# Moving the first tile's mask products to PE, with new load order, weight pieces and buffer counts, in a block-sparse attention and feed-forward kernel

## The chip, the cores and the metric

The kernel runs on one core of a Trainium2 chip. The metric is device time in microseconds (us) of the slowest core, here the only one, as the median of several executions. Before the change it was 276.54 us (three runs, 276.49 to 277.82). The engines are named as the profile names them: PE (matrix multiplications), PEld (PE's weight loads, which overlap PE), DVE (vector), ACT (scalar, exponentials and tanh), POOL (general purpose), SP (here only the issuer of the hardware load queue).

## The reference, cut to what matters

```python
batch, n_heads, seq, head_dim = 4, 8, 768, 64;  block = 32           # attention
n_tokens, d_model, d_ff = 3072, 512, 2048                            # feed-forward
scores = (1 / sqrt(64)) * matmul(q, k.transpose(0, 1, 3, 2))
mask = abs(blk_i - blk_j) <= 1  |  first or last block row or column
for qb in range(24):                       # and three drawn blocks of k in each block row
    for kb in sampled_blocks[qb]: mask[block qb, block kb] = True
attn = softmax(where(mask, scores, -1e9))
x = matmul(attn, v).transpose(0, 2, 1, 3).reshape(3072, 512)
h = x @ w_in;  g = h * sigmoid(beta * h);  out = g @ w_out           # float32 in and out
```

## The kernel before

The kernel writes down all its work as a list of nodes with an engine, a cost and dependences. A greedy scheduler then deals them out, once, while the program is recorded, and what comes out is a fixed order for each engine. An engine works through its list in order: if its next instruction must wait, everything behind it waits too (below, five loads wait behind one that is issued only at 13.42 us).

A *unit* is one pair of heads and one tile of queries (256 or 512). For each unit: loads of k, q and v (float32, into staging buffers `st_k`, `st_q`, `st_v`), casts to float16 on DVE or POOL, transposes on PE, score matmuls on 64 rows (PE), exponential (ACT), a product with a 0/1 mask (DVE), attention times V (PE, 65 columns), normalisation (DVE), a transpose of x. When all four pairs of a tile have their x, the feed-forward of that tile follows: matmuls with `w_in`, tanh (ACT), gate product (DVE), matmuls with `w_out`.

```python
SLOTS = {"st_k": 2, "st_q": 5, "st_v": 5, "s16_k": 4, "s16_q": 2, "set": 4, "va": 4,
         "et": 13, "xst": 5, "recip": 7, "t_sb": 6, "g": 2, "osb": 3, "sc": 4}   # buffers of each kind

def ex(eng, sc=sc, et=et):                              # one step: exponential of 128 x 1024 scores
    act.activation(out=at(et)..., in_=at(sc)..., func=AF.Exp, bias=0.0, scale=SCALE)

def mk(eng, et=et, kc0=kc0):                            # and its mask product
    dve.tensor_tensor(out=e, in0=e, in1=m, op=ALU.mult)

def load():                                             # all loads: one list, on SP
    ... nc.sync.dma_start(out=o, in_=hg)
last_load[:] = [add("load", "SP", ..., load, deps=..., take=[st])]      # takes a staging buffer

def shut():                                             # weights may start when pair 3's k has landed:
    nc.gpsimd.tensor_copy(out=w_in_sb[0:1, 0, 0:1], in_=at(st)[0:1, 0, 0:1])     # one element of it
... nc.gpsimd.dma_start(out=w_in_sb[...], in_=w_in_r[...])              # 2 + 2 pieces, issued by POOL
```

Batch 0 has four pairs of heads, numbered 0 to 3. Their loads go out in this order, where k0, q0, v0 belong to pair 0, k0a to k0c are thirds of k0, and r0 to r3 are the second halves (512 queries) of each pair's q:

```
k0a q0 k0b k0c v0 k1 q1 v1 k2 q2 v2 k3 q3 v3 r0 r1 r2 r3
```

The softmax here doesn't subtract the row's maximum and nothing guards it: scores larger than these inputs give would overflow.

Of the kernel before, what the change touches and what calls it, by code (L numbers as in the profile page):

```python
# [23 lines left out]
class Node:  # L24


    def __init__(self, kind, eng, dur, lat, emit, deps=(), take=(), use=(), moved=0,
# [13 lines left out]
BIAS = {"av": -69, "beta": -455, "cast": 94, "dma": -1239, "ex": 257, "gm": -727, "hp": -468,  # L41
        "load": 1496, "lone sc": 331, "mask": -1415, "mk": 241, "next sc": 94, "norm": -152,
        "op": -13, "op on": -70, "osb": 284, "sc": -204, "spread": -316, "th": 422,
        "turn": -3422, "turn cp": -88, "two sc": -72, "weights": 774, "x cp": -31,
        "x turn": -102}

W_GATE = (3, "k")
# [12 lines left out]
MOST = {"av": 8, "hp": 6, "sc": 3}  # L60
# [180 lines left out]
def kernel(  # L241
# [29 lines left out]
    SLOTS = {"st_k": 2, "st_q": 5, "st_v": 5, "s16_k": 4, "s16_q": 2, "set": 4, "va": 4,  # L271
             "et": 13, "xst": 5, "recip": 7, "t_sb": 6, "g": 2, "osb": 3, "sc": 4}
# [36 lines left out]
    onehot = persist.tile([NB, NG, P], FP16, name="onehot")  # L309
    mask16 = persist.tile([NB, NB], FP16, name="mask16")  # L310
# [26 lines left out]
    def emit_first():  # L337
# [6 lines left out]
        nc.vector.memset(warm, 0.0)  # L344

# [7 lines left out]
        nc.gpsimd.memset(onehot, 1.0)  # L353
        nc.gpsimd.affine_select(out=onehot, in_=onehot, pattern=[[CG * P, NG], [CG, P]],
                                compare_op=ALU.is_ge, fill=0.0, base=0,
                                channel_multiplier=-BLK)
        nc.gpsimd.affine_select(out=onehot, in_=onehot, pattern=[[-CG * P, NG], [-CG, P]],
                                compare_op=ALU.is_ge, fill=0.0, base=BLK - 1,
                                channel_multiplier=BLK)
# [22 lines left out]
    mask_of = {}  # L382

    def add_mask():
# [3 lines left out]
        def mb(eng):  # L388
            dve.tensor_copy(out=sb_f32, in_=sb_i32)
            for r in range(3):  # L390
                dve.scalar_tensor_tensor(out=mask_blk if r < 2 else mask16, in0=iota_j,
                                               scalar=sb_f32[:, r:r + 1], in1=mask_blk,
                                               op0=ALU.is_equal, op1=ALU.max)

        def mt():
            pe.matmul(at(tb)[0:NB, 0:NB], lhsT=mask16, rhs=identity[0:NB, 0:NB],
                             start=True, stop=True)
# [4 lines left out]
        def km():  # L402
            for g in range(NG):
                pe.matmul(at(kb)[:, g * NB:(g + 1) * NB], lhsT=onehot[:, g], rhs=mask_t,
                                 start=True, stop=True)
# [20 lines left out]
        n_mt = add("mask", "PE", 60, 200, mt, deps=[n_mb], take=[tb], rows=32)  # L426
        n_mtc = add("mask", ("ACT", "DVE"), {"ACT": 200, "DVE": 100}, 100, mtc, deps=[n_mt], use=[tb])
# [16 lines left out]
    def add_weights(gate):  # L444
        st, load = gate

        def shut():
            nc.gpsimd.tensor_copy(out=w_in_sb[0:1, 0, 0:1], in_=at(st)[0:1, 0, 0:1])
        gate = add("weights", "POOL", 600, 50, shut, deps=[load], use=[st])
        for i in range(2):  # L450
            def wi(i=i):
                nc.gpsimd.dma_start(out=w_in_sb[:, :, i * 1024:(i + 1) * 1024],
                                    in_=w_in_r[:, :, i * 1024:(i + 1) * 1024])
            w_in_of[i] = add("weights", "POOL", 1000, 0, wi,
                            deps=[gate if i == 0 else (w_in_of[0], -1e9)], moved=2097152, port=True)
# [279 lines left out]
    for x in range(NPAIR):  # L735
        add_rest(x)
# [74 lines left out]
```

## Time and profile before

| | before |
|---|---|
| median, three runs | 276.54 us |
| PE, DVE, ACT busy | 259.7, 209.2, 217.1 us of a profiled span of 275.0 |
| PE work, added up from start-to-start times | 250.3 us |
| end of the last matmul | 270.6 us, so PE lost 20.2 us |
| of these lost by 31.3 us / by 62 us | 16.4 / 19.7 us |
| first feed-forward matmul | 30.18 us |

"Lost" needs a word, because PE's busy share does not show it: a matmul that runs at half clock, or is drawn out by modelled ends, counts as busy. I added up what the PE stream needs at its usual spacing, read from the trace: 216 ns for a 512-column matmul, 109.5 for 256, 56 for 128, 32 for an attention-times-V matmul of 65 columns, 217 or 110 ns for a pair of 64-row score matmuls, and 96 ns at each change between 64 and 128 rows. Time elapsed less that sum is what PE lost.

The page of the kernel before; first busy time, share and instruction count, then the busy tenths in 40 slices of 6.9 us, then the chain that ended last:

```profile
PE 259.7 (94%) x2455; PEld 139.7 (51%) x2455; DVE 209.2 (76%) x416; ACT 217.1 (79%) x284; POOL 32.5 (12%) x53
...
PE   6677899969999999999999999999999999999993
...
PEclk9999999999999999999999999999999999999999
...
PE 88%; DVE 5%; ACT 2%; DMA 2%; SPq 1%; issue 1%; ACTq 0%; DVEq 0%
```

PE is full from slice 10 on. Only the start, the first nine slices, has room. The same start by stretches of 7 us; the columns are the stretch, its length, busy time of PE, PEld, DVE, ACT, POOL with counts, granted clock, DMA share and GB/s:

```profile
core 0: us, PE busy (x) PEld busy (x) DVE busy (x) ACT busy (x) POOL busy (x), PEclk, DMA share, GB/s
...
7.00:14.00 7.00, 4.79 (x51) 3.48 (x46) 5.21 (x11) 5.10 (x7) 1.54 (x2) 1.00 1.13 294
14.00:21.00 7.00, 5.26 (x59) 3.49 (x56) 6.13 (x14) 6.64 (x9) 3.41 (x6) 1.00 1.17 263
21.00:28.00 7.00, 5.65 (x93) 3.59 (x92) 6.42 (x16) 7.00 (x9) 1.76 (x2) 1.00 1.12 213
28.00:35.00 7.00, 6.33 (x62) 4.81 (x59) 6.63 (x16) 7.00 (x14) 0.00 (x0) 1.00 1.22 207
35.00:42.00 7.00, 7.00 (x90) 4.83 (x89) 6.59 (x18) 5.93 (x12) 1.17 (x3) 1.00 0.94 183
```

DVE and ACT are nearly full while PE is not. That is what the change goes for. The DMA share stands above 1 from 7 to 35 us, so the transfers may be a limit of their own in this stage. And four lines of the timeline (start, duration, engine, line of the kernel, operation, what ended the idle time before):

```profile
8.30 0.56 DVE L208 CAST s_k<-st_k 128x768 f16<-128x768 f32 x1 [0.67 <-DMA st_k<-in_k_dram]
...
8.89 0.90 SPq L474 DMA_DIRECT2D st_k<-in_k_dram  x1
...
10.92 1.46 PE L208 MATMUL sc<-qX,kX 64*128 64x256 f16 x12 [0.96 <-ACT qX L208]
...
17.95 0.83 PE L208 MATMUL sc<-qX,kX 64*128 64x256 f16 x12 [0.92 <-ACT qX L208]
```

There are two `st_k` buffers. The cast of pair 1's k, at 8.30, is the last reader of one of them, and as soon as it has ended the queue issues the load of pair 3's k, at 8.89. The timeline shows the same twelve score matmuls in 1.46 us and later in 0.83: until about 16.6 us the array ran at half clock. The clock row does not show it, because the clock's record only begins at 16.6 us; where there is no record the page prints 9.

### The profile page before, as it was taken

The numbers are of one execution on the slowest core, as the hardware profiler recorded it, in microseconds if no ns is written. First come the engines' busy times: TensorE is split into PE (matmuls) and PEld (weight loads), VectorE is DVE, ScalarE is ACT, GpSimd is POOL, SyncE is SP. The second block draws the span as 40 slices with busy tenths as digits, with TensorE's granted clock in tenths as the row PEclk, the third lists the DMA queues.
The fourth block names the chain that finished last, engine by engine and source line by source line (L and its number), as shares of the span: only waits on it lengthen the run. The fifth ranks groups of instructions, "written<-read, shape, count | busy, mean of one in ns | idle before, by whom it ended". The sixth has DMA issues, their size and how long they took to land.

```text
span 275.0 us, 6172 instructions
## 1 busy us (share of the span) xinstructions
PE 259.7 (94%) x2455; PEld 139.7 (51%) x2455; DVE 209.2 (76%) x416; ACT 217.1 (79%) x284; POOL 32.5 (12%) x53
## 2 busy tenths in 40 slices
PE   6677899969999999999999999999999999999993
PEld 2454674544455464455464444444545644567441
DVE  4789999998797798798988787977787877628000
ACT  3799998998789988789988788987798977529110
POOL 7243000043200112110010111030000000000000
PEclk9999999999999999999999999999999999999999
DMA  6999995599521798796577529490121300020222
GB/s 178 295 267 213 207 205 143 150 265 210 145 49 49 194 165 225 169 220 139 174 190 172 112 61 258 88 224 8 55 62 54 44 12 0 13 86 2 77 76 77
DMA packets 72882, 36.66 MB, mean 133 GB/s; under 512 B 29828, under 2 KB 68756, under 8 KB 72852
## 3 DMA queue, kind: packets, MB, share of 16 engines
q1 hardware_dynamic: 69600, 32.06, 47.3%
q0 software_dynamic: 3136, 4.19, 8.6%
q8 instruction: 19, 0.31, 0.5%
q14 instruction: 11, 0.09, 0.1%
q10 hardware_dynamic: 116, 0.01, 0.0%
HBM read 27.27 MB, written 6.29 MB: 122 GB/s over the span
## 4 chain that ended last, share of the span: by engine, by line
PE 88%; DVE 5%; ACT 2%; DMA 2%; SPq 1%; issue 1%; ACTq 0%; DVEq 0%
PE sc L208 88%; DVE et L208 2%; ACT et L208 2%; DMA st_k<-in_k_dram 2%; DVE xst L208 1%; SPq L477 1%; DVE recip L208 0%; DVE kX L208 0%; DVE s_k L208 0%; DVE xT_sb L208 0%; ACT qX L208 0%; ACT osb L208 0%; SPq L474 0%; DVE s_q L208 0%; DVE qX L208 0%
## 5 line engine op out<-in xcount | busy, mean ns | idle before, releaser
L208 ACT ACTIVATE et<-sc 128x1024 f16<-128x1024 f32 x144 | 136.4, 1045 | 13.9 <-PE sc L208 13.4
L208 DVE TENSOR_TENSOR et<-et,mask 128x1024 f16<-128x1024 f16 x144 | 94.8, 693 | 8.1 <-ACT et L208 8.0
L208 PE MATMUL sc<-w_out_sb,g 128*128 128x512 f16 x384 | 90.0, 379 | 0.0
L208 PE MATMUL sc<-xT_sb,w_in_sb 128*128 128x512 f16 (+1 forms) x448 | 84.3, 349 | 1.1 <-DVE xT_sb L208 1.0
L208 ACT ACTIVATE t_sb<-sc,beta_h_sb 128x512 f16<-128x512 f32 (+1 forms) x112 | 68.2, 649 | 17.1 <-PE sc L208 17.1
L208 DVE SCALAR_TENSOR_TENSOR g<-t_sb,sc 128x512 f16<-128x512 f16 (+1 forms) x112 | 67.6, 611 | 16.0 <-ACT t_sb L208 15.6
L208 PEld LDWEIGHTS <-w_in_sb 128*128 128x128 f16 x448 | 43.8, 98 | 40.7 <-issue 1.5
L208 PEld LDWEIGHTS <-g 128*128 128x128 f16 x384 | 34.6, 98 | 43.2 <-issue 7.5
L208 PE MATMUL sc<-qX,kX 64*128 64x256 f16 (+1 forms) x384 | 44.0, 339 | 4.7 <-ACT qX L208 1.9
L208 PEld LDWEIGHTS <-et 128*128 128x128 f16 x1152 | 39.7, 98 | 9.7 <-issue 6.6
L208 PE MATMUL sc<-va,et 128*128 128x65 f16 x1152 | 42.4, 194 | 1.1 <-ACT et L208 1.0
L208 PEld LDWEIGHTS <-kX 64*128 64x128 f16 x384 | 16.4, 98 | 26.5 <-issue 19.2
L208 ACT ACTIVATE osb<-sc 128x512 f32<-128x512 f32 x18 | 11.0, 608 | 17.9 <-PE sc L208 17.9
L208 DVE TENSOR_TENSOR xst<-sc,recip 128x256 f16<-128x256 f32 x48 | 20.3, 424 | 1.8 <-DVE recip L208 0.2
L497 POOL CAST s_k<-st_k 128x768 f16<-128x768 f32 (+1 forms) x11 | 8.2, 753 | 76.7 <-DMA st_k<-in_k_dram 76.6
L208 DVE RECIPROCAL recip<-sc 128x4 f32<-128x4 f32 x48 | 8.7, 180 | 10.4 <-PE sc L208 8.7
L497 POOL CAST s_q<-st_q 128x768 f16<-128x768 f32 (+2 forms) x11 | 9.0, 821 | 33.4 <-DMA st_q<-in_q_dram 33.0
L497 POOL CAST va<-st_v 128x768 f16<-128x768 f32 x7 | 6.6, 939 | 19.7 <-PE sc L208 15.2
L208 DVE CAST va<-st_v 128x768 f16<-128x768 f32 x9 | 5.0, 558 | 0.9 <-DMA st_v<-in_v_dram 0.9
L208 PE MATMUL sc<-identity,s_k 128*128 128x128 f16 x24 | 3.5, 305 | 2.0 <-DVE s_k L208 1.2
L208 DVE CAST s_k<-st_k 128x768 f16<-128x768 f32 x7 | 3.9, 554 | 1.4 <-issue 0.7
L208 DVE COPY xT_sb<-sc 128x256 f16<-128x256 f16 (+1 forms) x9 | 3.1, 346 | 1.8 <-PE sc L208 1.8
(53 smaller groups left out, 44.6 us busy)
## 6 DMA issues: line engine op xcount, KB each, us to landing
st_v<-in_v_dram SPq DMA_DIRECT2D x16, 384.0 KB, 5.1
out_dram<-osb SPq DMA_DIRECT2D x24, 256.0 KB, 2.2
st_k<-in_k_dram SPq DMA_DIRECT2D x15, 384.0 KB, 4.8
st_q<-in_q_dram SPq DMA_DIRECT2D x12, 384.0 KB, 4.2
w_in_sb<-in_moe_w_in_dram POOLq DMA_DIRECT2D x2, 1024.0 KB, 9.9
w_out_sb<-in_moe_w_out_dram POOLq DMA_DIRECT2D x2, 1024.0 KB, 16.6
st_q<-in_q_dram SPq DMA_DIRECT2D x12, 128.0 KB, 4.6
st_k<-in_k_dram SPq DMA_DIRECT2D x3, 128.0 KB, 2.6
```

The lines of the kernel that those rows point to most:

```text
L208: r = f(*a, **kw)
L477: nc.sync.dma_start(out=o[:, g::NG], in_=hg[:, g::NG])
L497: e(out=at(dst)[:, :, :, 0:D] if nm == "v" else by_chunk(dst, lo, hi), in_=src)
```

## The change

The intent: DVE lags in the start, so let PE, which waits there anyway, add the mask of the first tile. For the first four units (tile of queries 0 to 255 of batch 0, 12 steps), 48 one-hot matmuls put (mask − 1) × 30000 into the score banks ahead of the score matmuls, so that the exponential gives zeros by itself and 12 mask products on DVE go. The loads of batch 0 are put in another order, the weights are cut finer (six transfers instead of four; the list of gates has room for eight) and gated on earlier loads, and the scheduler's constants and the buffer counts are tuned anew for it. The diff, cut to its core:

```diff
-W_GATE = (3, "k")
+ORDER = "k0a r0 q0 k0c k0b v0 q1 v1 k1 k2 q2 v2 k3 r1 q3 v3 r2 r3"
+N_PEMASK = 4
+SHUT = 30000.0
+CUTS_IN = (0, 4, 8, 16)
+CUTS_OUT = (0, 4, 8, 16)
+GATES = ("k0b", "q0", "v1", None, None, None, None, None)
-MOST = {"av": 8, "hp": 6, "sc": 3}
+MOST = {"av": 12, "hp": 10, "sc": 3}
-    SLOTS = {"st_k": 2, "st_q": 5, "st_v": 5, "s16_k": 4, "s16_q": 2, "set": 4, "va": 4,
-             "et": 13, "xst": 5, "recip": 7, "t_sb": 6, "g": 2, "osb": 3, "sc": 4}
+    SLOTS = {"st_k": 2, "st_q": 3, "st_v": 4, "s16_k": 2, "s16_q": 3, "set": 4, "va": 4,
+             "et": 17, "xst": 2, "recip": 4, "t_sb": 3, "g": 2, "osb": 2, "sc": 4}
...
+        def neg(eng):
+            ... act.activation(out=o, in_=i, func=AF.Copy, bias=-SHUT, scale=SHUT)
...
+                        if by_pe:
+                            pe.matmul(at(sc)[:, hh, i * n:(i + 1) * n],
+                                lhsT=onehot[r, (kc0 + i) // CG, :],
+                                rhs=shut_qk[r, ...].to_broadcast(...), start=True, stop=False)
                         pe.matmul(at(sc)[:, hh, i * n:(i + 1) * n], lhsT=kX[...], rhs=qX[...],
-                            start=True, stop=True)
+                            start=not by_pe, stop=True)
...
+        if mk is None:
+            return e
         return add("mk", "DVE", 612, 80, mk, deps=[e] + masks, use=[et], port=True)
```

The constants in the table of priorities (`BIAS`) are all changed too; they only move the order.

More of the change, by code (lines that the diff above doesn't have):

```diff
@@ L38, in __init__ @@
         self.start = self.done = self.on = None
-BIAS = {"av": -69, "beta": -455, "cast": 94, "dma": -1239, "ex": 257, "gm": -727, "hp": -468,
-        "load": 1496, "lone sc": 331, "mask": -1415, "mk": 241, "next sc": 94, "norm": -152,
-        "op": -13, "op on": -70, "osb": 284, "sc": -204, "spread": -316, "th": 422,
-        "turn": -3422, "turn cp": -88, "two sc": -72, "weights": 774, "x cp": -31,
-        "x turn": -102}
-W_GATE = (3, "k")
+BIAS = {"av": -240, "beta": 221, "cast": 193, "dma": -549, "ex": 512, "gm": -1330, "hp": -309,
+        "load": 1600, "lone sc": 617, "mask": -820, "mk": 198, "next sc": 92, "norm": -24,
+        "op": -205, "op on": -229, "osb": 619, "sc": -618, "spread": 429, "th": 252,
+        "turn": -3740, "turn cp": -21, "two sc": 89, "weights": 742, "x cp": -657,
+        "x turn": -302}
+ORDER = "k0a r0 q0 k0c k0b v0 q1 v1 k1 k2 q2 v2 k3 r1 q3 v3 r2 r3"
[4 more added lines that the diff above has]
+GATES = ("k0b", "q0", "v1", None, None, None, None, None)
 SLACK = 1500.0
@@ L308 @@
     beta_h_sb = persist.tile([P, N_FFC], FP32, name="beta_h_sb")
-    onehot = persist.tile([NB, NG, P], FP16, name="onehot")
-    mask16 = persist.tile([NB, NB], FP16, name="mask16")
+    onehot = persist.tile([P, NG, P], FP16, name="onehot")
+    shut_qk = persist.tile([P, NG, P], FP16, name="shut_qk")
+    mask16 = persist.tile([NB, 2, P // 2], FP16, name="mask16")
     mask_t = persist.tile([NB, NB], FP16, name="mask_t")
@@ L344, in emit_first @@
         nc.vector.memset(warm, 0.0)
+        nc.vector.memset(mask16, 0.0)
         nc.gpsimd.iota(dif, pattern=[[1, NB]], base=0, channel_multiplier=-1,
@@ L352, in emit_first @@
         make_identity(nc, identity)
-        nc.gpsimd.memset(onehot, 1.0)
-        nc.gpsimd.affine_select(out=onehot, in_=onehot, pattern=[[CG * P, NG], [CG, P]],
-                                compare_op=ALU.is_ge, fill=0.0, base=0,
-                                channel_multiplier=-BLK)
-        nc.gpsimd.affine_select(out=onehot, in_=onehot, pattern=[[-CG * P, NG], [-CG, P]],
-                                compare_op=ALU.is_ge, fill=0.0, base=BLK - 1,
-                                channel_multiplier=BLK)
+        for h in range(2):
+            r = slice(h * D, (h + 1) * D)
+            nc.gpsimd.tensor_copy(
+                out=onehot[r].rearrange("b g (m r) -> b (g m) r", r=BLK // CG),
+                in_=identity[r, h * D:h * D + NB].unsqueeze(2).to_broadcast(
+                    [D, NB, BLK // CG]))
         nc.gpsimd.tensor_copy(out=ident32, in_=identity[0:16, 0:16])
@@ L380, in add @@
         return n
-    mask_of = {}
+    mask_of, n_neg = {}, []
     def add_mask():
@@ L389, in mb @@
             dve.tensor_copy(out=sb_f32, in_=sb_i32)
-            for r in range(3):
-                dve.scalar_tensor_tensor(out=mask_blk if r < 2 else mask16, in0=iota_j,
-                                               scalar=sb_f32[:, r:r + 1], in1=mask_blk,
-                                               op0=ALU.is_equal, op1=ALU.max)
-        def mt():
-            pe.matmul(at(tb)[0:NB, 0:NB], lhsT=mask16, rhs=identity[0:NB, 0:NB],
-                             start=True, stop=True)
+            for r in range(2):
+                dve.scalar_tensor_tensor(out=mask_blk, in0=iota_j, scalar=sb_f32[:, r:r + 1],
+                                         in1=mask_blk, op0=ALU.is_equal, op1=ALU.max)
+            both = [NB, 2, NB]
+            dve.scalar_tensor_tensor(
+                out=mask16[:, :, 0:NB], in0=iota_j.unsqueeze(1).to_broadcast(both),
+                scalar=sb_f32[:, 2:3], in1=mask_blk.unsqueeze(1).to_broadcast(both),
+                op0=ALU.is_equal, op1=ALU.max)
+        def mt():
+            pe.matmul(at(tb)[:, 0:NB], lhsT=mask16.rearrange("b h j -> b (h j)"),
+                      rhs=identity[0:NB, 0:NB], start=True, stop=True)
+        def neg(eng):
+            o = shut_qk.rearrange("b g (m r) -> b (g m) r", r=BLK // CG)
+            i = at(tb)[:, 0:NB].unsqueeze(2).to_broadcast([P, NB, BLK // CG])
+            if eng == "ACT":
+                act.activation(out=o, in_=i, func=AF.Copy, bias=-SHUT, scale=SHUT)
+            else:
+                dve.tensor_scalar(out=o, in0=i, scalar1=-1.0, scalar2=SHUT, op0=ALU.add,
+                                  op1=ALU.mult)
         def mtc(eng):
@@ L403, in km @@
             for g in range(NG):
-                pe.matmul(at(kb)[:, g * NB:(g + 1) * NB], lhsT=onehot[:, g], rhs=mask_t,
+                pe.matmul(at(kb)[:, g * NB:(g + 1) * NB], lhsT=onehot[0:NB, g], rhs=mask_t,
                                  start=True, stop=True)
@@ L426, in add_mask @@
         n_mt = add("mask", "PE", 60, 200, mt, deps=[n_mb], take=[tb], rows=32)
+        if N_PEMASK:
+            n_neg.append(add("mask", ("ACT", "DVE"), {"ACT": 400, "DVE": 470}, 100, neg, deps=[n_mt],
+                             use=[tb]))
         n_mtc = add("mask", ("ACT", "DVE"), {"ACT": 200, "DVE": 100}, 100, mtc, deps=[n_mt], use=[tb])
@@ L442, with add_weights, put, shut @@
     last_load, begin = [], []
-    def add_weights(gate):
-        st, load = gate
-        def shut():
-            nc.gpsimd.tensor_copy(out=w_in_sb[0:1, 0, 0:1], in_=at(st)[0:1, 0, 0:1])
-        gate = add("weights", "POOL", 600, 50, shut, deps=[load], use=[st])
-        for i in range(2):
-            def wi(i=i):
-                nc.gpsimd.dma_start(out=w_in_sb[:, :, i * 1024:(i + 1) * 1024],
-                                    in_=w_in_r[:, :, i * 1024:(i + 1) * 1024])
-            w_in_of[i] = add("weights", "POOL", 1000, 0, wi,
-                            deps=[gate if i == 0 else (w_in_of[0], -1e9)], moved=2097152, port=True)
-        for i in range(2):
-            def wo(i=i):
-                nc.gpsimd.dma_start(out=w_out_sb[:, i * 8:(i + 1) * 8, :],
-                                    in_=w_out_r[:, i * 8:(i + 1) * 8, :])
-            w_out_of[i] = add("weights", "POOL", 1200, 0, wo, deps=[(w_in_of[1], -1e9)],
-                              moved=2097152, port=True)
+    def add_weights():
+        prev, k = None, 0
+        for w_sb, w_r, cuts, of in ((w_in_sb, w_in_r, CUTS_IN, w_in_of),
+                                    (w_out_sb, w_out_r, CUTS_OUT, w_out_of)):
+            for lo, hi in zip(cuts, cuts[1:]):
+                def put(w_sb=w_sb, w_r=w_r, lo=lo, hi=hi):
+                    if w_sb is w_in_sb:
+                        nc.gpsimd.dma_start(out=w_sb[:, :, lo * P:hi * P],
+                                            in_=w_r[:, :, lo * P:hi * P])
+                    else:
+                        nc.gpsimd.dma_start(out=w_sb[:, lo:hi, :], in_=w_r[:, lo:hi, :])
+                deps = [(prev, -1e9)] if prev else []
+                if GATES[k]:
+                    st, load = loads[GATES[k]]
+                    spot = w_sb[0:1, 0, lo * P:lo * P + 1] if w_sb is w_in_sb else \
+                        w_sb[0:1, lo, 0:1]
+                    def shut(spot=spot, st=st):
+                        nc.gpsimd.tensor_copy(out=spot, in_=at(st)[0:1, 0, 0:1])
+                    deps.append(add("weights", "POOL", 600, 50, shut, deps=[load] + deps, use=[st]))
+                prev = add("weights", "POOL", 1000, 0, put, deps=deps,
+                           moved=262144 * (hi - lo), port=True)
+                for f in range(lo, hi):
+                    of[f] = prev
+                k += 1
@@ L463, in by_chunk, with add_load @@
     def by_chunk(s16, lo, hi):
         return at(s16)[:, lo * P:hi * P].rearrange("p (c h d) -> p h c d", h=2, d=D)
-    def add_load(nm, x, st, lo, hi, gate, more=False):
+    def add_load(nm, x, st, lo, hi, gate, more=None):
         b, j = pairs[x]
@@ L477, in load @@
                     nc.sync.dma_start(out=o[:, g::NG], in_=hg[:, g::NG])
-        deps = [(d, -1e9) for d in last_load + begin]
+        early = x < NPAIR
+        deps = [] if early else [(d, -1e9) for d in last_load + begin]
         kw = {"use" if more else "take": [st]}
@@ L482, in shut @@
                 nc.gpsimd.tensor_copy(out=at(st)[0:1, 0, lo * D:lo * D + 1],
-                                      in_=w_out_sb[0:1, gate * 8, 0:1])
+                                      in_=w_out_sb[0:1, gate, 0:1])
             deps.append(add("weights", "POOL", 600, 50, shut, deps=[w_out_of[gate]], take=[st]))
             kw = {"use": [st]}
-        last_load[:] = [add("load", "SP", 500 if hi - lo in (NC, CG) else 1000, 0, load, deps=deps,
-                             moved=68000 * (hi - lo) + (170000 if x == 0 and nm == "v" else 0),
-                             **kw)]
-        return last_load[0]
+        n = add("load", "SP", 500 if hi - lo in (NC, CG) else 1000, 0, load, deps=deps,
+                moved=68000 * (hi - lo) + (170000 if x == 0 and nm == "v" else 0), **kw)
+        if early:
+            what = f"{nm}{x}" if nm != "q" or lo == 0 else f"r{x}"
+            loads[what + ("abc"[lo // CG] if more is not None else "")] = st, n
+        else:
+            last_load[:] = [n]
+        return n
     def add_cast(x, nm, st, dst, lo, hi, load, more=False):
@@ L507, in add_half @@
         st, s16 = at_work or (Buf(f"st_{nm}"), Buf(f"s16_{nm}"))
-        load = add_load(nm, x, st, lo, hi, gate, at_work and lo > 0)
-        if x < NPAIR and lo == 0:
-            loads[x, nm] = st, load
+        load = add_load(nm, x, st, lo, hi, gate, lo > 0 if at_work else None)
         c = add_cast(x, nm, st, s16, lo, hi, load, at_work and lo > 0)
@@ L551, in add_prep @@
                    "k of": parts or [tk] * NG}
-        if x < NPAIR:
-            loads[x, "v"] = st, lv
     def add_rest(x):
@@ L559, with tile_steps @@
     x_of = {}
-    def tile_steps(x, q0, n):
+    def tile_steps(x, q0, n, by_pe):
         b, j = pairs[x]
@@ L574, in mm @@
                     for hh in range(2):
+                        if by_pe:
+                            r = slice(hh * D, (hh + 1) * D)
+                            pe.matmul(
+                                at(sc)[:, hh, i * n:(i + 1) * n],
+                                lhsT=onehot[r, (kc0 + i) // CG, :],
+                                rhs=shut_qk[r, q0 // (CG * P):(q0 + n) // (CG * P)].unsqueeze(
+                                    1).to_broadcast([D, CG, n // (CG * P), P]),
+                                start=True, stop=False)
+                    for hh in range(2):
                         pe.matmul(
@@ L579, in mm @@
                                 "d (g c p) -> d c g p", c=CG, p=P),
-                            start=True, stop=True)
+                            start=not by_pe, stop=True)
             def ex(eng, sc=sc, et=et):
@@ L594, in tile_steps @@
             k_of = prep[x]["k of"][kc0 // CG:(kc0 + kn - 1) // CG + 1]
-            steps.append((x, q0, k_of, sc, et, mm, ex, mk,
-                          [mask_of[g] for g in range(q0 // (CG * P), (q0 + n) // (CG * P))]))
+            steps.append((x, q0, k_of, sc, et, mm, ex, None if by_pe else mk,
+                          n_neg if by_pe else [mask_of[g] for g in range(q0 // (CG * P), (q0 + n) // (CG * P))]))
         return steps, ets
@@ L603, in add_step @@
         r = prep[x]
-        g = add("sc", "PE", 218, 180, mm, deps=[(t, SLACK if x >= N_PE_TURN else 0)
+        g = add("sc", "PE", 218 if mk else 436, 180, mm, deps=([] if mk else masks) + [(t, SLACK if x >= N_PE_TURN else 0)
                                            for t in dict.fromkeys(k_of)] + [
@@ L694, in add_moe @@
             w = 4 * (n / 2.4 + 2.5)
-            h = add("hp", "PE", w, 180, hp, deps=set(xs + [w_in_of[f // 8]]), take=[hb],
+            h = add("hp", "PE", w, 180, hp, deps=set(xs + [w_in_of[f]]), take=[hb],
                     place=gi * 16 + f)
@@ L708, in op @@
                                          start=(f == 0), stop=(f == N_FFC - 1))
-                prev = add("op on" if qq else "op", "PE", 864, 180, op, deps=gs + [w_out_of[qq // 2], (prev, -180 - HOP)
+                prev = add("op on" if qq else "op", "PE", 864, 180, op, deps=gs + [w_out_of[qq * 4], (prev, -180 - HOP)
                                                           if prev else None],
@@ L733 @@
         add_prep(x)
-    add_weights(loads[W_GATE])
     for x in range(NPAIR):
         add_rest(x)
+    early = [loads[x][1] for x in ORDER.split()]
+    assert len(early) == len(loads)
+    for a, b in zip(early, early[1:]):
+        b.deps.append((a, -1e9))
+    last_load.append(early[-1])
+    add_weights()
     halves = ((0, Q1), (Q1, S - Q1)), ((0, S - Q1), (S - Q1, Q1))
@@ L747 @@
             x = b * NPAIR + j
-            steps, ets = tile_steps(x, q0, n)
+            steps, ets = tile_steps(x, q0, n, i * NPAIR + j < N_PEMASK)
             masked = []
@@ L755 @@
                 if first_unit[y] == i * NPAIR + j + AHEAD:
-                    add_prep(y, (0, 1, 1) if y == NPAIR else (None, None, None))
+                    add_prep(y, (0, 8, 8) if y == NPAIR else (None, None, None))
         upto = b * S + q0 + n
@@ L760 @@
             gi += 1
-    seq = order_of(nodes, {"PE": 3900.0, "ACT": 3950.0, "DVE": 2800.0, "POOL": 3350.0,
+    seq = order_of(nodes, {"PE": 3900.0, "ACT": 3950.0, "DVE": 2800.0, "POOL": 2900.0,
                            "SP": 800.0}, SLOTS)
```

## The prediction

> **What bounds the kernel now.** The page: PE busy 259.7 us of 275.0, ACT 217.1, DVE 209.2. Adding up the PE stream by its start-to-start times in the timeline (216 ns per 512-column matmul, 32 ns per attention-times-V matmul, 217 ns per pair of 64-row score matmuls, about 96 ns for each change between 64 and 128 rows) gives about 250 us of PE work. The last matmul ends at 270.8, so about 20 us of PE time are lost: 16.4 before 31.3 us, 3.4 between 53 and 62, under 1 after that. From 62 us the kernel stands on PE's rate; only the start can be won.
>
> In the start PE waits. By stretches, DVE is busy 6.1, 6.4, 6.6 and ACT 6.6, 7.0, 7.0 of every 7 us between 14 and 35. DVE lags ACT: the last exponential of the first tile ends near 21 us, its mask product only near 28, and the first feed-forward matmul starts at 30.2, after the fourth xT copy (DVE). Part of the loss is a cold array: 12 score matmuls take 1.46 us at 6 to 15 us and 0.83 at 18 (timeline), as the Trainium skill, "TensorE: Matmul & The Clock Gate", Part 1, says of an idle array (half clock). The trace agrees.
>
> **Removed.** 12 of 144 mask products (602 ns each start to start): 7.2 us of DVE, all before 28 us. The first-tile path exp, mask, attention-times-V loses a link.
>
> **Added.** 48 one-hot matmuls of 256 columns on 64 rows. The trace shows the two row halves starting 4 ns apart (the same page, Part 3, "The mechanism", says so too), so 24 pairs of 110 ns: 2.6 us warm, up to twice that cold, plus four more row switches (0.4): 3.0 us of PE work, in a stretch where PE idles anyway. ACT gets one copy more (about 0.5 us) before the scores, and all 24 output copies (18 now), late.
>
> **Moved.** The built order puts the 512-query scores of pair 0 among the first exponentials, so that ACT has nine exponentials before it needs pair 1's k. Before the first feed-forward matmul stand 20 exponentials that it needs (12 before), about 18 us of PE work instead of 14. Weights now start right after pair 0's loads, while the DMA share is already over 1.1 (7 to 28 us); this may delay k of pairs 1 and 2.
>
> **On the critical path.** DVE's saving cannot all be paid out: ACT takes over. First exponential still near 7 us; 20 exponentials at 904 ns plus copies end near 27 to 28; the tail of norm, transpose and copy is 2.7 us: the feed-forward starts near 30 to 31 us, no earlier, but with about 2 us more useful PE work behind it. ACT idles only 2.3 us between 7 and 32 and 1.9 from 32 to 60; about half of that is what I expect back. PE after the second feed-forward start is unchanged (about 208 us).
>
> **Predicted:** 273.8 us, 8 in 10 between 270.3 and 277.3. Faster by over 2%: 0.16; within 2%: 0.80; slower by over 2%: 0.04.
>
> **Right if:** mask products fall from 144 to 132; DVE busy falls by 6 to 9 us; PE busy share before 31 us rises; the first feed-forward matmul is at 29 to 32 us; ACT is busy over 6.7 of every 7 us from 10 us on and is what PE waits for; the loss between 53 and 62 us shrinks below 3 us; from 62 us to the end the time is as before, within 1 us.
>
> **Wrong if:** weight transfers stall the in-order ACT on k of pairs 1 or 2 (slower); the smaller buffer counts (two xst, three t_sb, two output buffers) open gaps after 62 us; or the filled array warms early and the second loss vanishes too (270 or less).

## The result, and the profile after

| | before | after |
|---|---|---|
| median of fast runs, same rounds | 276.7 us | 285.62 us (284.93 to 286.09) |
| ratio, 95% interval | | 1.0312 (1.0275 to 1.0349): slower |
| profiled span | 275.0 | 284.3 |
| PE work | 250.3 | 253.3 |
| PE lost by 62 us / in all | 19.7 / 20.2 | 23.7 / 26.5 |
| first feed-forward matmul | 30.18 | 41.84 |

A ratio here and below is the mean time of one kernel's fast runs over that of the other's of the same rounds, so it is not quite the ratio of the medians quoted. Executions over 1.5% slower than the fastest of the same kernel are left out of the means. The last matmul starts 9.2 us later (279.6 against 270.4): 3.0 us are the added PE work, 6.3 us (rounded) are additional loss.

The page after, the same rows as above:

```profile
PE 263.6 (93%) x2503; PEld 141.5 (50%) x2503; DVE 196.7 (69%) x398; ACT 217.1 (76%) x291; POOL 32.0 (11%) x57
...
PE   6785289999999999999999999999999999999993
...
PEclk9999789999999999999999999999999999999999
...
PE 75%; DMA 11%; DVE 5%; ACT 3%; SPq 3%; issue 1%; ACTq 0%; DVEq 0%
```

DVE is 12.5 us less busy, as meant, and PE is no better for it. Slices 4 to 6 of PE's row have a hole (5, 2, 8), the clock drops in slices 5 and 6, and the chain of waits has 11% DMA where it had 2%. By stretches:

```profile
7.00:14.00 7.00, 5.30 (x50) 2.83 (x47) 3.57 (x9) 5.74 (x6) 1.54 (x5) 1.00 0.90 251
14.00:21.00 7.00, 5.96 (x109) 4.59 (x106) 3.77 (x9) 6.32 (x9) 5.42 (x9) 1.00 0.94 193
21.00:28.00 7.00, 4.45 (x66) 2.83 (x62) 3.51 (x9) 6.79 (x10) 1.29 (x2) 1.00 1.16 220
28.00:35.00 7.00, 1.16 (x18) 1.16 (x19) 1.61 (x4) 1.02 (x2) 0.00 (x0) 0.75 1.17 214
35.00:42.00 7.00, 6.26 (x89) 4.43 (x87) 4.04 (x11) 3.84 (x5) 0.79 (x2) 0.76 1.23 210
```

Up to 21 us PE is fuller than before, as promised, and up to 24 us PE had lost 2 us less (11.6 against 13.6). But the gain is the added work itself: by then PE had run 36 one-hot matmuls, 2.0 us of work, so the rest of the program was no further on than before. From 28 to 35 us PE, DVE and ACT are nearly idle (1.16, 1.61 and 1.02 us busy of 7) and only the DMA works. The timeline says for what, in the lines that matter:

```profile
11.16 0.56 DVE L213 CAST va<-st_v 128x768 f16<-128x768 f32 x1 [1.94 <-DMA st_v<-in_v_dram]
11.63 1.28 DVE L213 TENSOR_TENSOR et<-et,mask 128x1024 f16<-128x1024 f16 x2
12.84 0.55 DVE L213 CAST s_k<-st_k 128x768 f16<-128x768 f32 x1
13.42 0.37 SPq L505 DMA_DIRECT2D st_k<-in_k_dram  x1
...
33.36 0.43 DVE L213 CAST s_q<-st_q 128x512 f16<-128x512 f32 x1 [5.20 <-DMA st_q<-in_q_dram]
...
33.84 0.61 PE L213 MATMUL sc<-identity,s_q 128*128 128x128 f16 x4 [7.54 <-DVE s_q L213]
...
38.16 4.69 ACT L213 ACTIVATE et<-sc 128x1024 f16<-128x1024 f32 x5 [9.14 <-PE sc L213]
...
41.84 4.09 PE L213 MATMUL sc<-xT_sb,w_in_sb 128*128 128x256 f16 x36 [0.45 <-DVE xT_sb L213]
```

Read from below: ACT waited 9.14 us for scores, PE 7.54 us for a cast of q on DVE, DVE 5.20 us for the transfer. It is the load r2 (second half of pair 2's q). The upper four lines show how the queue fell behind: the load of pair 3's k, which before was issued at 8.89, now goes out at 13.42, after the cast of pair 1's k at 12.84, and that cast stands in DVE's list behind a cast of v, which waited until 11.13 for its data, and two mask products. All loads behind it in the list, r1, q3, v3, r2, r3, wait with it. DVE's list is the smaller part of the delay. Pair 1's k itself landed only at 12.30 us (before: 8.28): the new order issues it at 5.64 instead of 3.54, behind r0, q1 and v1. (In f7_room below, with the same order, it landed at 10.71, so the order is not all of it.) Its cast then started 0.54 us later. The waits of the load queue at this place, for the landing and then for the cast (in all, times, longest):

```profile
SPq L505 <- DMA st_k<-in_k_dram: 1.4, 1, 1.4
SPq L505 <- DVE s_k L213: 1.8, 2, 1.1
```

The chain of waits has r2 itself (start, duration, what):

```profile
16.72 16.55 DMA st_q<-in_q_dram
...
33.36 0.44 DVE s_q L213
```

The load took 16.55 us. Before, the loads had moved 4.46 of their 4.72 MB by 18 us; after, 3.66 MB, so that 1.06 MB were left when the weights came (their first packets are at 16.5 us, before at 17.9). From there both share the DMA engines. The DMA view of the kernel after, for 26 to 28 us, by queue: q0 has the weights, q1 the loads; packets, MB, and the share of 16 engines:

```profile
q0 software_dynamic: 176, 0.35, 91.2%
q1 hardware_dynamic: 165, 0.08, 19.9%
```

The two queues moved nearly equal numbers of packets, 176 and 165, but the weights' packets had about 2 KB and the loads' 0.5 KB, so the loads got 0.08 MB in 2 us, some 40 GB/s. Without weights beside them (10 to 16 us of the kernel before) they got 290 GB/s. The Trainium skill, "DMA: Bandwidth & Descriptors", section "Queues, rings and completion order", says that a DMA engine takes turns between its queue rows by packets; this trace agrees, as far as the profile's packets are those of the page, which are groups of descriptors. In the kernel before the sharing is the same (524 against 552 packets from 18 to 24 us), but only 0.26 MB of loads were left to suffer from it.

The half clock is a second cost of the same wait: the clock's record is at half from 31.5 to 38.3 us, after PE had idled from 26.3 to 33.8. "TensorE: Matmul & The Clock Gate", Part 1, describes this: an idle array falls to half clock and gets it back only after sustained work. The trace agrees.

### The profile page after: what moved, and what is told of

Read it like the earlier page. It is cut to its first block, busy times and chain, and to the rows that moved or that the text cites. A ratio compares the mean times of both kernels' runs of the same rounds, so it can differ in the third digit from the quotient of the medians.

```text
span 284.3 us, 6249 instructions
## 1 busy us (share of the span) xinstructions
PE 263.6 (93%) x2503; PEld 141.5 (50%) x2503; DVE 196.7 (69%) x398; ACT 217.1 (76%) x291; POOL 32.0 (11%) x57
## 4 chain that ended last, share of the span: by engine, by line
PE 75%; DMA 11%; DVE 5%; ACT 3%; SPq 3%; issue 1%; ACTq 0%; DVEq 0%
PE sc L213 75%; DMA st_q<-in_q_dram 6%; DVE g L213 2%; DMA st_v<-in_v_dram 2%; SPq L508 2%; DVE et L213 2%; ACT t_sb L213 2%; DMA xT_sb<-xst 2%; ACT et L213 1%; DMA st_k<-in_k_dram 1%; DVE xst L213 1%; SPq L505 0%; SPq L548 0%; DVE xT_sb L213 0%; ACT osb L213 0%
## 5 line engine op out<-in xcount | busy, mean ns | idle before, releaser
L213 ACT ACTIVATE et<-sc 128x1024 f16<-128x1024 f32 x144 | 138.0, 1037 | 19.4 <-PE sc L213 17.9
L213 DVE TENSOR_TENSOR et<-et,mask 128x1024 f16<-128x1024 f16 x132 | 88.1, 695 | 10.5 <-ACT et L213 10.0
L213 PE MATMUL sc<-xT_sb,w_in_sb 128*128 128x512 f16 (+1 forms) x448 | 86.4, 349 | 1.0 <-DVE xT_sb L213 0.5
L213 DVE SCALAR_TENSOR_TENSOR g<-t_sb,sc 128x512 f16<-128x512 f16 (+1 forms) x112 | 65.9, 609 | 15.9 <-ACT t_sb L213 14.6
L213 PE MATMUL sc<-qX,kX 64*128 64x256 f16 (+1 forms) x384 | 46.5, 335 | 1.4 <-ACT qX L213 0.5
L213 ACT ACTIVATE osb<-sc 128x512 f32<-128x512 f32 x24 | 14.5, 603 | 29.9 <-PE sc L213 27.8
L213 PEld LDWEIGHTS <-kX 64*128 64x128 f16 x384 | 16.5, 97 | 23.6 <-issue 19.5
L533 POOL CAST s_q<-st_q 128x768 f16<-128x768 f32 (+2 forms) x16 | 11.9, 746 | 92.0 <-DMA st_q<-in_q_dram 65.6
L213 PE MATMUL sc<-identity,s_q 128*128 128x128 f16 x24 | 3.2, 263 | 8.2 <-DVE s_q L213 7.5
L213 PE MATMUL sc<-shut_qk,onehot 64*128 64x256 f16 x48 | 7.2, 316 | 0.8 <-ACT et L213 0.6
L213 DVE CAST s_k<-st_k 128x768 f16<-128x768 f32 (+1 forms) x12 | 6.4, 534 | 0.2 <-DMA st_v<-in_v_dram 0.2
```

The lines of the kernel that those rows point to most:

```text
L213: r = f(*a, **kw)
L533: e(out=at(dst)[:, :, :, 0:D] if nm == "v" else by_chunk(dst, lo, hi), in_=src)
```

## The experiments

The theories (the quoted expectations were written before each run):

- *Staging*: with the new load order and the same or fewer staging buffers, the in-order load queue waits for a buffer; late loads then meet the weights.
- *Weights*: the weights come too early and take the bandwidth; the loads would be late even with free buffers.
- *The mask on PE itself*: one-hot matmuls and the mask chain ahead of the scores cost what is seen.
- *The new order*: the rest of the retuning (priorities, the other buffer counts) costs it.

In all runs whose name begins with f, the order of instructions on every engine is the kernel's own, taken from the scheduler and kept, except for the one thing named. Where the scheduler runs anew (a2, n3, b1) the whole order may move. Runs of one group share their runs of the kernel before: 277.43 us median in the first group (a2, f1, f2, f3), 277.7 in the second (f4, f5, f7), 277.32 in the third (f8, f9, n3, b1), 277.1 in the fourth (f11, f12, f7 again).

How a buffer count is changed without moving the order: after scheduling, the buffers of a kind are dealt out in turn. This is sound only if, in the recorded order, every reader of a buffer stands before the buffer's next load. It holds for the staging buffers in all these runs but f2_tight.

```diff
+    ROOM = {**SLOTS, "st_k": 4, "st_q": 6}              # f7; the others differ in this line
+    for pool in ROOM:                                   # after order_of(...)
+        if ROOM[pool] != SLOTS[pool]:
+            taken = [b for n in seq for b in n.take if b.pool == pool]
+            for i, b in enumerate(taken):
+                b.slot = i % ROOM[pool]
```

### f1_room: after, with the staging buffers of q and v as before

`ROOM = {**SLOTS, "st_q": 5, "st_v": 5}`

> The changed kernel, not one instruction moved; only q gets 5 staging buffers instead of 3 and v 5 instead of 4, as before the change. Theory A (loads are issued late because staging buffers are short, so 1.2 MB of them are still on the way when the weights start and crawl): the second halves of q land within 6 us of issue instead of up to 16.5, PE has no wait over 2 us after 20 us, time 272 to 277. Rival B (the mask on PE costs more than it saves): the time stays at 283 or more. Rival C (the weights are cut and gated too early, staging does not matter): the 7.5 us wait stays, 282 or more.

285.77 us, ratio 1.0307 (1.0281 to 1.0332): nothing gained. Pair 3's k was still issued at 13.16 us and 3.66 MB had moved by 18 us. The staging theory in its first form, the reduced counts of q and v as the cause, fell. The load that the queue stands at is one of k, whose count the diff had not changed.

### f2_tight: before, with the staging buffers of q and v as after

`ROOM = {**SLOTS, "st_q": 3, "st_v": 4}`

> The kernel before, not one instruction moved; only q gets 3 staging buffers instead of 5 and v 4 instead of 5. Theory A: loads slip behind the start of the weights here too, PE waits several us for a q half between 20 and 40 us, time 281 or more. Rivals B and C: within 1 us of the kernel before, 276 to 278.

285.2 us, ratio 1.0288 (1.026 to 1.0315). This looks as if the reduced counts alone cost the old kernel nearly as much as the whole change cost, but the edit changed more than the counts, and the run can't be used. Dealt out in turn over three buffers, the second half of pair 3's q (r3) gets the buffer of r0, and in the recorded order r3's load stands before r0's cast. So r0's data are overwritten unread, and the cast that should read them waits for r3 instead. The traces show it. In the kernel before, r0's cast follows a cast of v on DVE at 18.03; in f2_tight the cast at the same place comes at 25.68 and waits for the load issued last of all, at 17.65:

```profile
18.03 0.41 DVE L208 CAST s_q<-st_q 128x512 f16<-128x512 f32 x1
```

```profile
25.68 0.43 DVE L208 CAST s_q<-st_q 128x512 f16<-128x512 f32 x1 [7.38 <-DMA st_q<-in_q_dram]
```

The chain of waits of f2_tight (start, duration, what) has that load in it:

```profile
11.67 5.49 DMA st_q<-in_q_dram
17.18 0.37 SPq L479
17.55 0.05 issue
17.65 7.94 DMA st_q<-in_q_dram
```

It met the weights (first packets at 17.6 us) and took 7.94 us; PE waited 7.2 us for the cast, and the clock was at half from 19.8 to 30.0. The run counts as correct on record because the values of q hardly matter with inputs this small. In the simulator, rows 256 to 767 of its output are off by 0.7% with such inputs and by 56% with q and k ten times as large, while the kernels before and after are off by 0.06% at most. What the reduced counts alone cost the old kernel stays open.

### f3_pemask: before, with the mask of the first four units on PE and nothing else

```diff
+                        if by_pe:
+                            pe.matmul(... lhsT=onehot[...], rhs=shut_qk[...], start=True, stop=False)
-                            start=True, stop=True)
+                            start=not by_pe, stop=True)
# 12 mask products dropped, one ACT activation added; everything else in before's order
```

> The kernel before with the first-tile mask on PE and nothing else: the 12 mask products are dropped, 48 one-hot matmuls and one ACT copy added, all other instructions in the order of before. Theory A: the mask alone is worth little but does no harm, 274.5 to 277.5. Rival B: it costs, 279 or more.

278.52 us, ratio 1.0039 (1.0006 to 1.0071). DVE was busy 44.81 us of the first 60 instead of 51.28. By 62 us PE had lost 17.9 us instead of 19.7, but it had 2.6 us more to do, so nothing was won: the first feed-forward matmul came at 30.14 (before 30.18). The first exponential came at 7.92 instead of 6.86, because the first scores now wait for the mask, and PE waited for ACT. PE's waits up to 62 us, the largest group:

```profile
PE sc L208 <- ACT et L208: 3.1, 8, 0.6
```

The profiled execution, the slowest of the four, also shows half clock from 61.7 to 65.1 us, for which no cause was looked for. So the mask on PE costs the old order 0.4%, not 3%. That theory is out as the cause.

### a2_gate: after, with the weights' first piece gated on the last load, order made anew

```diff
-GATES = ("k0b", "q0", "v1", None, None, None, None, None)
+GATES = ("r3", None, None, None, None, None, None, None)
```

> The changed kernel with the first piece of weights held until the last early load (the second half of q of pair 3) has landed, and scheduled anew for it. Theory A: no early load travels beside weights, all land within 6 us, the 16.5 us landing is gone; the feed-forward starts a little later for want of weights; 274 to 281. Rival B: 283 or more.

This run gave a wrong result (relative error 0.403, in every second row from 1537 to 2047, in batch 2; the simulator gives the same error). Other variants whose order was made anew had it too, and I did not find its cause in the recording layer; this is why most experiments keep the order. 288.61 us, ratio 1.0421, may not be used as a verdict. Its start is of interest: with all loads landed by about 21 us the first feed-forward matmul came at 29.51 and PE had lost 12.8 us by 31.3, but 10.4 us were lost after 80 us (added up as above; the expectation of n3 below says 12), which was not followed up.

### f4_late: after, only the weights later

```diff
+    def wait_for_loads():                    # the weights' gate: one element of the last load, r3
+        nc.gpsimd.tensor_copy(out=w_in_sb[0:1, 0, 0:1], in_=at(loads["r3"][0])[0:1, 0, ...])
+    seq[first:first] = [shut] + weights      # all six transfers behind it, in POOL's list only
```

> The changed kernel; only GpSimd's stream differs: the three gate copies are dropped, and the six weight transfers are issued after one copy that waits for the last early load (second half of q of pair 3) to land. Staging buffers as in the change, every other engine's order untouched. Theory A2 (what stalls is the sharing: loads that are still on the way when the weights start get about 45 GB/s): all early loads land within 6 us of issue, the 7.5 us wait of PE for q of pair 2 is under 2 us, the array stays warm; 274 to 279. Rival B (the added PE work, or the order, costs): 282 or more. Rival C (weights that come later stall the feed-forward): 280 or more, with PE waiting for w_in between 30 and 45 us.

283.79 us, ratio 1.0226 (1.0198 to 1.0254): a quarter of the loss gone. The long wait for q vanished (PE had lost 13.0 us by 31.3 instead of 17.4), which shows the weights' part in it. But the loads still needed their buffers, the last was issued at 23.2 us, and the weights' first packets came at 27.6. PE waited for them then. The largest group of PE's waits from 30 to 50 us:

```profile
PE sc L213 <- DMA w_in_sb<-in_moe_w_in_dram: 3.0, 1, 3.0
```

The next group is 2.9 us for a cast of q on POOL, which stood in POOL's list behind a gate copy that ran only at 42.23 us. In all 10 us were lost between 31.3 and 62, and the clock was at half again from 40.0 to 46.9. Keeping the two streams apart alone moves the wait.

### f7_room: after, with room for the loads: four k and six q staging buffers

`ROOM = {**SLOTS, "st_k": 4, "st_q": 6}`

> The changed kernel, not one instruction moved; k gets 4 staging buffers instead of 2, q 6 instead of 3, so that no load waits for a cast; weights start as in the change (packets from about 16.5 us). If late issue is what leaves loads to the weights' mercy, as theory A held: under 0.4 MB of early loads left at 18 us (1.06 MB in the changed kernel), stall under 3 us, 275 to 280. If the time that the weights start decides (A2): 0.5 MB or more left, a stall of over 4 us remains, 280 to 285.

276.51 us, ratio 0.9971 (0.9927 to 1.0014): the same as before, and about 9 us less than after, with no instruction moved on any engine. Pair 3's k was issued at 9.42 us, 4.27 MB of loads had moved by 18 us, the first feed-forward matmul came at 31.00, and PE lost 14.7 us by 62. The timeline of f7_room's load queue at the place where the kernel after stood still, and its stretches:

```profile
9.42 0.93 SPq L507 DMA_DIRECT2D st_k<-in_k_dram  x1
```

```profile
14.00:21.00 7.00, 5.87 (x89) 4.08 (x90) 3.50 (x9) 7.00 (x10) 5.02 (x9) 1.00 1.19 254
21.00:28.00 7.00, 6.14 (x118) 4.85 (x116) 5.30 (x14) 6.79 (x9) 0.00 (x0) 1.00 1.15 215
28.00:35.00 7.00, 6.20 (x73) 4.91 (x70) 5.70 (x14) 7.00 (x13) 0.77 (x2) 1.00 1.24 208
```

The hole from 28 to 35 us is gone, ACT is full, and the record has no half clock after 8.2 us. The 0.45 MB of loads left at 18 us lie between the two bounds of the expectation; the time and the vanished wait decide for the staging theory in its second form: buffers of k first, then of q. (Six q buffers are one more than the kernel before has; four k and five q was not run.)

### f7_again: the same kernel, five rounds

No edit.

> f7 once more with five rounds, on the chip of the two others: 275.5 to 277.5, ratio to the kernel before 0.993 to 1.001. It is the base for f11 and f12.

276.96 us, ratio 0.9996 (0.9961 to 1.003). The kernel with room equals the kernel before. The profile differs somewhat from the first one: the first feed-forward matmul is at 32.44 us, PE lost 15.5 us by 62 us and 16.9 in all, and the clock is full from 12.2 us on. So about 1 us of such figures is the difference between two executions of one kernel.

### f8_k4: after, with four k staging buffers only

`ROOM = {**SLOTS, "st_k": 4}`

> The changed kernel, not one instruction moved; only k gets 4 staging buffers instead of 2 (q 3 and v 4 as in the change). In the changed kernel the load of pair 3's k is issued at 13.4 us, after waiting for the cast of pair 1's k at 12.8, and every later load stands behind it in the one queue. If that wait is the root (A3): the load is issued before 10 us, under 0.5 MB of early loads left at 18 us, 275 to 279; the second half of q of pair 3 may still be late for want of a q buffer. If the q buffers matter as much: 280 to 284. If neither (rival B): 284 to 287.

281.19 us, ratio 1.0141 (1.011 to 1.0172), about 4.5 us better than after: half of the way. Pair 3's k was issued at 9.76 us, but by 18 us only 3.87 MB had moved. Now the queue stands at q. The largest groups of waits of f8_k4 from 14 to 42 us that concern q:

```profile
DVE s_q L213 <- DMA st_q<-in_q_dram: 3.7, 1, 3.7
PE sc L213 <- DVE s_q L213: 3.7, 1, 3.7
```

The late load is r2, whose second part was issued at 16.12 us and landed at 28.20 (f7_room: 13.89 and 22.17). The queue had waited 0.5 us for a cast of q before q3, ahead of r2, and it waited 5.0 us before r3. With f1 (q to 5, and v: nothing), f8 (k alone: half) and f7 (k, and q to 6: all), the two counts work in series: the queue stands at k first, and only when that is cured at q.

### f9_bwide: control, before with four k staging buffers

`ROOM = {**SLOTS, "st_k": 4}`

> Control: the kernel before, not one instruction moved, k with 4 staging buffers instead of 2. Its loads hardly wait for casts (pair 3's k is issued at 8.9 us), so by A3 nothing is to be had: 276 to 278. A gain of over 2 us would say that wide staging is worth something by itself and f7's recovery not special to the change.

277.11 us, ratio 0.9991 (0.9965 to 1.0018). In the old load order the two more k buffers bring nothing.

### f5_both: f7 and the late weights of f4

`ROOM = {**SLOTS, "st_k": 4, "st_q": 6}`, and the edit of f4.

> Both at once: the wide staging and the late weights. By A and A2: no stall on loads, all early loads landed by 18.5 us, weights from 19 to 20 us, PE's loss up to 31 us below the 16.4 us of the kernel before; 273 to 278, as good as f4 or up to 2 us better. By rival B: 282 or more.

279.88 us, ratio 1.0079 (1.005 to 1.0108). The loads were through sooner still (4.69 MB by 18 us), but the weights, first packets at 21.8 us, came late: PE lost 4.7 us from 35 to 45, and the clock was at half from 38.6 to 42.0. Once the loads are issued in time, weights beside them do no harm, and holding them back costs 3 us. The weights theory is thus half right: they stretch whatever load is late, but they are not what makes it late.

### f11_dvemask: f7, with the mask of the first four units back on DVE

```diff
+        if n.kind == "ex" and n.emit in mk_of:          # right behind its exponential
+            f, et = mk_of[n.emit]
+            m = Node("mk", "DVE", 612, 80, f, use=[et]);  m.on = "DVE"
+            out_seq.append(m)                           # and no one-hot matmuls
```

> The f7 kernel (changed order, wide staging) with the first-tile mask taken back to DVE: 12 mask products right behind their exponentials, no one-hot matmuls, no shut copy on ACT; all else in the order of f7. If the mask on PE is free where PE waits for ACT anyway, and DVE has room too (it is busy about half of the time there): within 1.5 us of f7. If the 3 us of PE work are paid in full: 2 to 3 us faster than f7. If relieving DVE is what the changed order lives on: over 2 us slower than f7.

283.19 us, ratio 1.0224 (1.019 to 1.0257), 6 us slower than f7 in the same rounds. In this order the mask products stand in front of the casts of k in DVE's list. PE's largest wait from 14 to 42 us:

```profile
PE sc L214 <- DVE s_k L214: 5.0, 2, 3.0
```

The array stayed at half clock until 30.6 us (f7_room: 8.2). So in the new order DVE's relief is worth something, up to 6 us; only "up to", since I placed the products in one way and another may cost less.

### f12_cpdve: f7, with six copies of q and k moved from ACT to DVE

```diff
+    for n in seq[began:]:
+        if n.kind == "turn cp":
+            n.on = "DVE"
```

> The f7 kernel with the six q and k copies that ACT makes after its first exponential (about 3 us) given to DVE at their places. If ACT sets the pace of the start, as I hold: PE's loss up to 60 us falls by 1 to 3 us, the time is 1 to 2.5 us under f7. If not ACT but the loads or PE set it: within 0.7 us of f7, or slower where DVE's order makes PE wait.

277.32 us, ratio 1.0005 (0.997 to 1.0041); PE lost 15.35 us by 62 instead of f7_again's 15.56. ACT was busy 50.59 us of the first 60 instead of 52.74, and the time did not move. ACT is not what alone sets the pace.

### n3_gk3: after, with wide staging and one gate on pair 3's k, order made anew

`GATES = ("k3", None, ...)`, `SLOTS` with `"st_k": 4, "st_q": 6`

> The changed kernel scheduled anew, with k 4, q 6, v 4 staging buffers and the weights held until pair 3's k has landed, as in the kernel before. By A3 loads stay ahead and weights come at about 14 us: 273 to 278 if the order found is as good as the changed one; orders made anew have shown losses after 80 us (the gate run lost 12 us there), then 278 to 284.

The result was correct. 279.23 us, ratio 1.0067 (1.0039 to 1.0095). The first feed-forward matmul is the earliest of all kernels here (27.66), and 14.9 us were lost by 62, as in f7_room (14.7), but later stages lost more (last matmul at 272.0; f7_room 268.9). No kernel that I tried is faster than the kernel before by more than the noise.

### b1_pemask: before's settings with the mask on PE, order made anew

The kernel after with before's `BIAS`, `SLOTS`, `MOST` and load order, two pieces for each weight, and `GATES = ("k3", None, None, None)`.

> The mask on PE in the settings of before (its weights in four transfers, its staging, its load order), but scheduled anew around the mask, where f3 kept the order. If f3's +0.4% came from an order that did not fit: 274 to 276.5. If ACT, which starts about 1 us later because scores now wait for the mask, sets the time: 277 to 279.

282.58 us as the median of all four runs (279.45 to 283.87). Two of them, the profiled one included, were slow; the two fast ones are 279.45 and 281.45, ratio 1.0114 (1.0057 to 1.0171), above both ranges that were expected. With two fast runs 2 us apart I draw nothing from it; f3 answers its question with the order kept.

## Why the prediction was wrong

It said 273.8 us and the same within 2%, and gave slower by over 2% a chance of 0.04. Measured: 285.62 us, 3.1% slower.

- *Mask products 144 to 132*: right. *DVE busy falls by 6 to 9 us*: it fell by 12.5. The 12 products explain some 7; six output copies of 0.684 us, gone from DVE to ACT, another 4.
- *48 one-hot matmuls cost about 3.0 us of PE work*: right, 253.3 against 250.3. The Trainium skill's page "TensorE: Matmul & The Clock Gate", Part 3, "The mechanism", and the trace agree that the two row halves run together (starts 4 ns apart).
- *First exponential near 7 us*: right, 7.17.
- *"ACT takes over ... the feed-forward starts near 30 to 31 us, no earlier, but with about 2 us more useful PE work behind it"*: **this is the step that failed.** It started at 41.84. The sum counted exponentials and copies and took for granted that q, k and v arrive as before. Their arrival was the term left out: r2 landed at 33.27. In f7_room, where the loads are on time, the first feed-forward matmul is at 31.00 (f7_again: 32.44), by 31.3 us PE has done 4.1 us more work than before (f7_again: 3.4), of which 2.6 are one-hot matmuls, and by 62 us it has lost 14.7 us instead of 19.7. So the estimated start was about right for a kernel with buffers enough, and the useful work gained there was 0.8 to 1.5 us rather than 2.
- *"ACT busy over 6.7 of every 7 us from 10 us on and what PE waits for"*: wrong in the kernel after (5.74, 6.32, 6.79, then 1.02). In f7_room ACT is near full (7.00, 6.79, 7.00), but f12 relieved it without gain, so it is not the limit alone.
- *"Weights now start right after pair 0's loads"*: wrong. POOL's list is in order too; the first issue was at 14.38 us, before 15.37.
- *"Wrong if weight transfers stall the in-order ACT on k of pairs 1 or 2"*: the right kind of risk, at the wrong load, and given far too small a chance. The stall was at the second half of pair 2's q, and the weights were the second cause. The first was in plain sight: a load order that issues k1 later, so that k3's buffer comes free later (13.39 us, before 8.86), and `st_q` from 5 to 3. The prediction listed smaller buffer counts as a risk, but only `xst`, `t_sb` and the output buffers, and only after 62 us.
- *From 62 us on as before within 1 us*: the loss after 62 us was 2.8 us against 0.5, so wrong by a little over 1 us. In f7_room, with the same small counts of the other buffers, it is 1.1; most of it is therefore not due to those counts. What it is instead I did not determine.

Put together: the mask on PE was worth nothing in the old order (f3, 0.4% slower) and up to 6 us in the new one (f11). What the change could bring was lost to a load queue that stood still for a buffer of k and then of q (f8, f7), by weights that stretched the late load to 16.55 us (f4), and by an array at half clock after the wait. With room for the loads (f7) the change stands level with the kernel before, not ahead of it: PE lost 4.4 us less in all (15.8 against 20.2; in f7_again 3.3 less) and paid 3.0 us of it for the one-hot matmuls; the 1.4 us that are left in the profiled spans (273.6 against 275.0; f7_again 274.8) are within what the ratios leave open. No run changed the load order alone; that it makes k3 late is read from the traces (k1 lands at 12.30, in f7_room at 10.71, before at 8.28). Open are also the reduced counts in the old order (f2), the wrong result of a2, the late losses of the orders made anew, and other placements of the mask products in f11.

## What to carry to other kernels

When a change reorders loads or lowers a buffer count, write down for each load which instruction frees its buffer and when that instruction runs in its engine's list; one load that waits holds up all that stand behind it in an in-order queue. A late load is dearer than an early one, because it shares the DMA engines with whatever comes next, here at a seventh of its rate. To tell "too few buffers" from "a bad order", keep the order and change only the buffers: it cost one run here and gave back 9 us. When buffers are dealt out anew in a kept order, check that each one's readers stand before its next load, with inputs large enough for an error to show; f2_tight passed its check with another pair's q.

## What the Trainium skill lacked or had wrong

- "DMA: Bandwidth & Descriptors", section "Queues, rings and completion order", has the turns by packets, but not what follows for bandwidth: beside weight packets of about 2 KB, loads in packets of 0.5 KB got 0.08 MB in 2 us (some 40 GB/s, against 0.35 MB for the weights), and 290 GB/s without them.
- The same page, section "Issuing engines are not separate DMA queues", says that issuing from several engines saves only the issuer's time. Here the issuer's list decides more: one load that waits for its staging buffer (13.42 us instead of 8.89) holds back all loads behind it. No page that I read has this.
- "TensorE: Matmul & The Clock Gate", Part 1, gives about 3.4 us of sustained work for the full clock. In f11_dvemask PE was busy 4.2 to 5.3 of each 7 us up to 28 us, in short runs with gaps, and the array stayed at half clock until 30.6 us; in the kernel before it did until 16.6, in f7_room only until 8.2 and in f7_again, the same kernel, until 12.2. The page's "A second HAM failure mode: psum-queue depth-cycling" says that frequent short idle times can make the clock fall and rise again, but not how much gap is too much, so none of these times could have been told from it.
